# Projecting the last full chunk by tokens in a planned attention and MLP kernel

## The chip, the cores and the metric

The kernel runs on one core of a Trainium2 chip. A core has a matrix engine (PE, with its weight loads shown as PEld), a vector engine (DVE), a scalar engine (ACT), a general engine (POOL), an engine that here only issues transfers (SP), and 16 DMA engines. Each engine works through its own list of instructions in order; semaphores hold an instruction back until what it reads is written and what it overwrites has been read. The metric is the device time of one execution in microseconds, as the median of several runs.

## The reference

Attention with a polynomial feature map comes first, then an MLP whose activation is a rational function:

```python
a = einsum('rd,bhsd->bhsr', S1, x);  b = einsum('rd,bhsd->bhsr', S2, x)
phi(x) = outer product of a and b, flattened            # 8 x 8 = 64 features
kv  = einsum('bhsf,bhsd->bhfd', phi(k), v);  z = phi(k).sum(over s)
x   = (phi(q) @ kv) / (phi(q) . z + 1e-6)               # per head, heads joined: (4352, 128)
h = x @ w_in                                            # (4352, 2048)
P = a[0] + a[1]*h + a[2]*h**2 + a[3]*h**3
Q = 1 + |b[0]|*|h| + |b[1]|*h**2
out = (P / (Q + 1e-6)) @ w_out                          # (4352, 128)
```

There are 4 batches of 4 heads with 1088 tokens and a head width of 32. q, k, v, w_in and w_out are float32; w_in is 128 x 2048 and w_out 2048 x 128. The output is float32.

## The kernel before

**Chunks.** Of each batch 1024 tokens are worked on in two chunks of 512. The first chunk of batch 0 is split into 128 and 384 tokens. The 64 tokens left over in each batch make one last chunk of 256, the remainder. In the loops these are n = 0 to 9: n = 8 is the last full chunk (batch 3, second half) and n = 9 the remainder. In the names of steps the label runs one lower: `0`, `0b`, `1` to `7` for n = 0 to 8, and `8` for the remainder.

**Attention.** For each batch the keys are transposed and turned into features, and PE sums them with the values (L498). For each chunk the queries are transposed (`q tr`), copied (`q ev`), projected (`q abc`), divided by the denominator on DVE (`q dpr`, `q dsum`, `q dinv`, `q scale`), multiplied out (`q prod`), transposed again (`qp tr`), copied (`qp ev`) and multiplied with the sums (`x mm`, L685). The copy `x ev` (L729) gives xT, 128 features by the chunk's tokens.

**MLP.** The 2048 hidden units are 16 blocks of 128. A group g is some blocks of one chunk: n = 7 has groups 15 and 16, n = 8 groups 17 and 18, each of 8 blocks, that is 128 x 4096 values; the remainder has groups 19 to 22 with 8, 4, 3 and 1 blocks. The steps of a group, by their names in the plan:

- `h g,s`: PE multiplies w_in with xT in float32 (L831), two blocks of 512 tokens (four of 256) into one of two PSUM buffers `h_ps`. s counts the blocks, so (18,4) is the third pair of group 18.
- `hev g,s`: the cast of that buffer to bfloat16 `hb` (L838), by ACT, or by DVE for the pairs that CASTS names.
- `abs` (L850), `sq` (L858), `odd` (L862), `oddt` (L868 with hb): DVE makes |h|, h squared, a3 h^2 + a1, and that times h. What is added (`+Q`, `+P`) is added by DVE (L920) or by accumulating DMAs that POOL issues (L924), as PLANS says.
- `ln` (L872) and `exp` (L875): ACT takes Ln of the denominator and Exp of its negative, so u = 1/Q.
- `n5` (L868 with u): DVE multiplies y with u.
- `pr` and `py`: PE multiplies with w_out and adds up in the one PSUM buffer `out_ps`. For groups 13 to 22 the constant a0 is not added to y; instead u itself is projected with w_out scaled by a0 (`w_out_0`), that is `pr`, and y with the other scaled copy (`w_out_b`), that is `py`.

**The two forms of the projection.** Line 888 holds w_out still and streams 512 tokens, so the result has tokens in columns. It is copied (`oev`, L893), transposed by PE (`otr`, L898), copied again (`otev`, L903) and stored. By tokens (L883) the values of 128 tokens are held still and 128 columns of w_out are streamed, so the result has its tokens in partitions; one copy (L957) and the store follow. BY_TOKEN lists the chunks that do it so: here the remainder alone.

**Scaling w_out.** w_out is loaded as float32 into a buffer of the ring `y`. ACT makes w_out_b from it in two halves (`w1`, L435), DVE makes w_out_0 in two halves (`w0`, L436).

**Order.** Every step is entered in a plan with an engine, an estimated duration, what it comes after, a rank, and buffers that it takes and gives back. The planner (`listed`) once put the steps in an order by these numbers; that order is written out as ORDER, and `issue` follows it. Estimated durations, ranks, lags and buffer counts therefore act only through ORDER: each engine's instructions are issued in it. Buffers are handed out in that order too.

**Fillers.** HOT lists groups of matmuls of zeros (L1049) whose result nobody reads. They take a `w_ps` buffer like a transpose, and stand in PE's list where ORDER has them.

Of the kernel before, what the change touches and what calls it, by code (L numbers as in the profile page):

```python
# [55 lines left out]


class Plan:
# [66 lines left out]
def kernel(  # L125
# [37 lines left out]
    BY_TOKEN = (9,)  # L163
# [19 lines left out]
    plan = Plan(BUFS)  # L183
# [87 lines left out]
    ld = {}  # L271
# [813 lines left out]
```

## Time and profile before

| | us |
|---|---|
| median of 3 runs (246.26 to 246.79) | 246.72 |
| the profiled execution | 247.33 |
| its span, first to last instruction | 245.3 |
| busy in the span: PE (weight loads apart) | 239.0 |
| DVE | 223.5 |
| ACT | 219.8 |
| POOL | 48.4 |
| PE in zero matmuls of L1049, 49 of them | 11.8 |

Busy time of PE counts from the start of a matmul to a modelled end. Rows of the timeline merge instructions of one kind: start, time from the start of the first to the end of the last, engine, line, operation, output and inputs, shape, count. Two rows of one engine may overlap by a tenth or more, since an instruction begins before the one ahead has ended; what one costs its engine is therefore taken from start to start. The chain of waits is followed back from the last instruction, at each step to what released it.

### The profile page before, as it was taken

What the parts mean: (1) busy time and instruction counts of PE and PEld (TensorE: products, weight loads), DVE (VectorE), ACT (ScalarE), POOL (GpSimd) and SP (SyncE); (2) the same over time, 40 slices, a digit from 0 to 9 for tenths busy, and PEclk for the clock granted to TensorE, in tenths of its full rate; (3) what the DMA queues carried; (4) which work ended last, traced back from release to release, by engine and by line L of the source; (5) the groups of instructions that cost most, each with busy time, mean ns of one, the idle gap of its engine ahead of it and who ended that gap; (6) DMA issues with size and microseconds to landing.
All of it is one profiled execution on the core that took longest, in us unless ns stands there. A gap on an engine that the chain in (4) does not pass through costs nothing.

```text
span 245.3 us, 3066 instructions
## 1 busy us (share of the span) xinstructions
PE 239.0 (97%) x1148; PEld 138.4 (56%) x1148; DVE 223.5 (91%) x242; ACT 219.8 (90%) x199; POOL 48.4 (20%) x70
## 2 busy tenths in 40 slices
PE   8998999999999999999999999999999999999986
PEld 4887667665556486456464554435444444755453
DVE  0747889999999999999999999999999999999792
ACT  3237799898979998899999999999999999999993
POOL 7800021010121503011112111231311112111100
PEclk9999999999999999999999999999999999999999
DMA  6897706855869999999799999999999999999822
GB/s 159 266 319 178 259 12 123 165 169 97 150 117 184 174 191 222 212 196 179 128 181 180 184 175 176 229 170 187 184 187 191 212 191 172 193 194 188 158 88 64
DMA packets 22206, 42.96 MB, mean 175 GB/s; under 512 B 5536, under 2 KB 12720, under 8 KB 22064
## 3 DMA queue, kind: packets, MB, share of 16 engines
q0 software_dynamic: 8544, 31.74, 72.6%
q1 hardware_dynamic: 13360, 10.95, 14.6%
q8 instruction: 9, 0.15, 0.2%
q10 hardware_dynamic: 288, 0.08, 0.2%
q14 instruction: 5, 0.04, 0.0%
HBM read 8.82 MB, written 2.23 MB: 45 GB/s over the span
## 4 chain that ended last, share of the span: by engine, by line
PE 60%; ACT 35%; issue 3%; DVE 0%; ACTq 0%
PE h_ps L831 31%; ACT u L875 13%; ACT L L872 12%; PE w_ps L498 7%; ACT hb L838 6%; PE out_ps L888 4%; PE w_ps L463 3%; PE w_ps L627 3%; PE w_ps L685 2%; PE w_ps L673 2%; PE w_ps L617 2%; PE w_ps L454 1%; PE out_ps L359 1%; ACT q_pT L679 1%; ACT o_sb L893 1%
## 5 line engine op out<-in xcount | busy, mean ns | idle before, releaser
L831 PE MATMUL h_ps<-xT,w_in_sb 128*128 128x512 f32 (+3 forms) x320 | 126.3, 533 | 0.0
L831 PEld LDWEIGHTS h_ps<-xT,w_in_sb 128*128 128x128 f32 x320 | 55.5, 190 | 41.9 <-issue 31.9
L872 ACT ACTIVATE L<-u,kappa 128x4096 f32<-128x4096 bf16 (+6 forms) x23 | 66.2, 2884 | 0.1
L875 ACT ACTIVATE u<-L 128x4096 bf16<-128x4096 f32 (+6 forms) x23 | 64.3, 2801 | 0.1
L838 ACT CAST hb<-h_ps 128x1024 bf16<-128x1024 f32 (+3 forms) x53 | 54.5, 1051 | 4.8 <-PE h_ps L831 4.6
L924 POOL DMA_DIRECT2D u<-lin x17 | 20.8, 1224 | 120.4 <-DVE lin L858 29.0
L868 DVE TENSOR_TENSOR y<-y,u 128x4096 bf16<-128x4096 bf16 (+6 forms) x23 | 39.7, 1727 | 1.7 <-ACT u L875 1.6
L868 DVE TENSOR_TENSOR y<-y,hb 128x4096 bf16<-128x4096 bf16 (+6 forms) x23 | 39.5, 1725 | 0.0
L858 DVE TENSOR_TENSOR lin<-hb 128x4096 bf16<-128x4096 bf16 (+6 forms) x22 | 37.9, 1724 | 1.4 <-ACT hb L838 1.3
L888 PE MATMUL out_ps<-y,w_out_b 128*128 128x512 bf16 (+2 forms) x144 | 30.6, 355 | 0.2 <-DVE y L868 0.2
L924 POOL DMA_DIRECT2D y<-lin x15 | 19.0, 1268 | 59.5 <-DVE lin L865 27.0
L862 DVE TENSOR_SCALAR y<-lin,a_t 128x4096 bf16<-128x4096 bf16 (+6 forms) x23 | 24.6, 1068 | 0.3 <-ACT lin L856 0.2
L850 DVE TENSOR_SCALAR u<-hb 128x4096 int16<-128x4096 int16 (+6 forms) x23 | 21.6, 941 | 2.1 <-ACT hb L840 1.2
L888 PEld LDWEIGHTS <-w_out_b 128*128 128x128 bf16 x144 | 13.5, 98 | 16.0 <-issue 4.2
L498 PEld LDWEIGHTS w_ps<-v_aug,k_p 128*128 128x128 f32 x128 | 14.9, 192 | 1.4 <-ACT ab L470 0.8
L498 PE MATMUL w_ps<-v_aug,k_p 128*128 128x96 f32 x128 | 15.6, 276 | 0.0
L838 DVE CAST hb<-h_ps 128x1024 bf16<-128x1024 f32 x11 | 13.4, 1220 | 0.7 <-PE h_ps L831 0.7
L865 DVE TENSOR_SCALAR lin<-lin,a_t 128x4096 bf16<-128x4096 bf16 (+3 forms) x13 | 13.4, 1030 | 0.0
L673 PEld LDWEIGHTS w_ps<-ident,q_p 128*128 128x128 f32 x66 | 7.8, 141 | 7.5 <-issue 3.9
L1049 PE MATMUL w_ps<-const-float32-0.0 128*128 128x512 bf16 x49 | 11.8, 381 | 0.0
L679 ACT COPY q_pT<-w_ps 128x512 f32<-128x512 f32 (+2 forms) x18 | 10.9, 603 | 1.0 <-PE w_ps L673 1.0
L888 PE MATMUL out_ps<-u,w_out 128*128 128x512 bf16 x48 | 11.3, 379 | 0.0
(118 smaller groups left out, 226.6 us busy)
## 6 DMA issues: line engine op xcount, KB each, us to landing
u<-lin POOLq DMA_DIRECT2D x14, 1024.0 KB, 8.6
y<-lin POOLq DMA_DIRECT2D x13, 1024.0 KB, 9.5
v_aug<-in_v_dram SPq DMA_DIRECT2D x8, 256.0 KB, 4.9
out_dram<-oT SPq DMA_DIRECT2D x7, 256.0 KB, 7.5
kq<-in_k_dram SPq DMA_DIRECT2D x3, 512.0 KB, 4.7
kq<-in_q_dram SPq DMA_DIRECT2D x3, 512.0 KB, 7.7
u<-lin POOLq DMA_DIRECT2D x2, 768.0 KB, 7.0
w_in_sb<-in_moe_w_in_dram SPq DMA_DIRECT2D x1, 1024.0 KB, 6.6
```

The lines of the kernel that those rows point to most:

```text
L498: nc.tensor.matmul(kv_of((hp,))[:, 0], lhsT=lhs(hp), rhs=rhs(hp), start=(first and hp == hps[0]), stop=final, skip_group_check=True)
L831: nc.tensor.matmul(T["h", g, s][:, i * step:i * step + W], lhsT=w_in_sb[:, fi * 128:(fi + 1) * 128], rhs=T["xT", n][:, :W], start=True, st ...
L838: copy(out=T["t", g][:, s * W:(s + nsub) * W], in_=T["h", g, s][:, :nsub * W])
L850: nc.vector.tensor_scalar(out=u().bitcast(mybir.dt.int16), in0=ht().bitcast(mybir.dt.int16), scalar1=0x7FFF, scalar2=None, op0=AX.bitwise_and)
L858: nc.vector.tensor_mul(out=sq(), in0=ht(), in1=ht())
L862: nc.vector.tensor_scalar(out=y(), in0=sq(), scalar1=a_t[:, 3:4], scalar2=a_t[:, 1:2], op0=AX.mult, op1=AX.add)
L865: nc.vector.tensor_scalar(out=sq(), in0=sq(), scalar1=a_t[:, 0:1], scalar2=None, op0=AX.add)
L868: return lambda: nc.vector.tensor_mul(out=out(), in0=in0(), in1=in1())
L872: nc.scalar.activation(out=T["L", g][:, :gw], in_=u(), func=ACT.Ln, bias=1.0 + 1e-6, scale=kappa[:, 2:3])
L875: nc.scalar.activation(out=u(), in_=T["L", g][:, :gw], func=ACT.Exp, scale=-1.0)
L888: nc.tensor.matmul(T["o", n][:, :W], lhsT=w[:, fi, :], rhs=T[src, g][:, i * W:(i + 1) * W], start=(start and i == 0), stop=(stop and i == ...
L924: nc.gpsimd.dma_start(out=dst(), in_=src(), accum_op=AX.add, max_dma_last_dim=GW)
```

## The change

The full chunk n = 8 joins the remainder in BY_TOKEN. Its four projections (pr and py of groups 17 and 18) become 32 matmuls of 128 columns each, where they were 8 of 512; the copy to o_sb and four transposes behind them fall away, and one copy from `out_ps` takes the place of the copy from the transposes. One more cast, the second half of group 19, goes from ACT to DVE. The scalings of w_out come later in the order, because the planner now counts 700 ns more for the load; a `free u` step tells the planner that u is free once n5 and pr have read it. HOT has the same places but for the last three, 6, 4, 2 where 4, 4, 6 were, 47 matmuls of zeros where 49 were. All steps have new numbers, and ORDER is a new plan for them: the order differs on PE, DVE and ACT from about 16 us on, on SP only in the last stores, and on POOL in one place.

```diff
--- before.py
+++ after.py
@@ -17,42 +17,42 @@
 ORDER = [
-    0, 4, 5, 56, 2, 7, 9, 51, 6, 11, 1, 52, 53, 3, 13, 70, 8, 10, 54, 57, 15, 75, 71, 17, 12, 72, 59, 55, 58, 76,
-    14, 60, 19, 77, 21, 73, 16, 74, 23, 99, 80, 78, 25, 100, 18, 81, 101, 79, 27, 82, 102, 85, 20, 83, 61, 84, 29,
...
-    790, 800, 791, 788, 801, 723, 792]
+    0, 4, 5, 57, 2, 7, 9, 52, 6, 11, 1, 53, 54, 3, 13, 71, 8, 10, 55, 58, 15, 76, 72, 17, 12, 73, 60, 56, 59, 77,
+    14, 61, 19, 78, 21, 74, 16, 75, 23, 100, 81, 79, 26, 101, 18, 82, 102, 80, 28, 83, 103, 86, 20, 84, 62, 85, 30,
...
+    794, 681, 795, 791, 682, 793, 805, 703, 796, 806, 797]
@@ -158,10 +158,10 @@
     FIRST = [4, 4, 8]
     LAST = [8, 4, 3, 1]
     PLANS = {**{g: "QP" for g in range(4, 20)}, **{g:"QPz" for g in range(13,20)},5:"QP",3:"Q",4:"sQP",17:"Qz",19:"QPz",20:"z",21:"z",22:"z"}
-    CASTS = {18:(6,),16:(6,),14:(6,),12:(6,),17:(6,),13:(6,),15:(6,),11:(6,),10:(6,),8:(6,),9:(6,)}
+    CASTS = {18:(6,),16:(6,),14:(6,),12:(6,),17:(6,),13:(6,),15:(6,),11:(6,),10:(6,),8:(6,),9:(6,),19:(4,)}
     PACKED = (0, 9)
-    BY_TOKEN = (9,)
-    HOT = [6, 2, 5, 5, 6, 11, 4, 4, 6]
+    BY_TOKEN = (8,9)
+    HOT = [6, 2, 5, 5, 6, 11, 6, 4, 2]
     ZEROS = 8
     assert d_model == 128 and H == 4 and D == 32 and R == 8 and REM == 64 and J % JC == 0
 
@@ -286,6 +286,7 @@
     ld["q", 0, 1] = load("SP", lambda e: load_main(e, "q_sb", q, 0, 1), 256, rank=-94)
     second = dict(mains(1))
     ld["wo"] = load("SP", load_wo, 800, rank=-93, take=["y"])
+    ld["wo"] = plan.add("ST", 1, lambda: None, after=[ld["wo"]], rank=-93, lag=700, name="w_out")
     ld["k", 1] = load("SP", second["k"], 512, 1, rank=-91, take=["kq"])
     ld["v", 1] = load("SP", second["v"], 512, NP, rank=-90, take=["v_aug"])
     ld["q", 1] = load("SP", second["q"], 512, 1, rank=-89, take=["kq"])
@@ -946,8 +947,10 @@
         p = used(add_up("+P", y, sq, [p, v, dq0], g - 0.3, give=give("sq")), "sq")
         p = used(plan.add("DVE", tt, mul(y, y, u), after=[p, e], rank=g + 0.55, give=[] if z else give("u"), name=f"n5 {g}"), "u")
         o = plan.add("PE", len(fis) * pw, lambda: project("y", w_out_b, first and not z, final), after=[p, rt] + c_w[:1 + (fis[-1] >= NF // 2)], rank=g + 0.56,
-                     take=["out_ps"] if first and not z else [], give=give("u", "y") if z else give("y"), name=f"py {g}")
+                     take=["out_ps"] if first and not z else [], give=give("y"), name=f"py {g}")
         used(o, "y")
+        if z and not packed:
+            plan.add("ST", 1, lambda: None, after=[p, rt], rank=g + 0.56, give=["u"], name=f"free u {g}")
         if packed and final:
             for kind, (tag, _, eng, _) in KINDS.items():
                 plan.add(eng, 1, lambda: None, after=T[kind, "used", n], rank=g + 0.6, give=[tag], name=f"give {tag} {n}")
```

66 rows, old and new, of the table ORDER are left out of this document.

## The prediction

> **What bounds the kernel now.** I read the busy shares first, then the chain of waits, then the stages, then each engine's rows in order of time.
>
> ```profile
> span 245.3 us, 3066 instructions
> ...
> PE 239.0 (97%) x1148; PEld 138.4 (56%) x1148; DVE 223.5 (91%) x242; ACT 219.8 (90%) x199; POOL 48.4 (20%) x70
> ...
> PE 60%; ACT 35%; issue 3%; DVE 0%; ACTq 0%
> ```
>
> Three engines are over 89% busy, so no one of them is "the" bound. The chain lies on PE and then on ACT. The stages say the same (columns: stretch, its length, busy time of PE, weight loads, DVE, ACT and POOL with instruction counts, granted clock, DMA share, GB/s):
>
> ```profile
> 180.00:200.00 20.00, 20.00 (x70) 9.07 (x69) 19.70 (x14) 20.00 (x13) 3.54 (x3) 1.00 1.05 197
> ...
> 225.00:230.00 5.00, 5.00 (x26) 2.33 (x24) 3.74 (x4) 5.00 (x4) 0.86 (x1) 1.00 0.86 160
> ...
> 235.00:240.00 5.00, 3.85 (x55) 3.33 (x56) 4.82 (x12) 4.97 (x8) 0.00 (x0) 1.00 0.15 56
> ```
>
> From 180 to 200 us PE and ACT are full and DVE lacks 0.30 us. At 225 to 230 DVE has 1.26 us free, and at 235 to 240 PE, though its clock stays at 1.00. So work taken from one engine is worth something only as far as the other two come earlier too, and a gap that is worth filling exists on DVE near the end.
>
> **The change, part by part.** The span is 245.3 us; this execution took 247.33, of which 2.03 lie around the span. The median of the runs is 246.72, 0.61 less; the changes below are put on the median.
>
> *Projection by tokens.* Chunk 8 has four projections (pr and py of groups 17 and 18). Each was 8 matmuls of 512 columns and becomes 32 of 128. PE rows near the end show both kinds (columns here and below: start, duration, engine, line and operation, operands and shape, count; in brackets the idle time before and what ended it):
>
> ```profile
> 228.14 1.89 PE L888 MATMUL out_ps<-y,w_out_b 128*128 128x512 bf16 x8
> 229.87 0.60 PE L898 MATMUL w_ps<-ident,o_sb 128*128 128x128 f32 x4
> 230.31 1.89 PE L888 MATMUL out_ps<-u,w_out 128*128 128x512 bf16 x8
> ...
> 235.87 1.06 PE L883 MATMUL out_ps<-w_out,u 128*128 128x128 bf16 x16
> 236.77 1.06 PE L883 MATMUL out_ps<-w_out_b,y 128*128 128x128 bf16 x16
> ```
>
> Start to start, 8 of the long ones take 1.73 us (228.14 to 229.87) and 16 of the short ones 0.90 (235.87 to 236.77), 56 ns each. So 128 short ones take 7.2 us where 32 long ones took 6.9: +0.3 us. The four transposes (229.87 to 230.31) go: -0.44. For PE that is nothing, if the 56 ns hold; the upper bound is one weight load for each matmul, unhidden:
>
> ```profile
> L883 PEld LDWEIGHTS <-u 128*128 128x128 bf16 x32 | 1.9, 98 | 0.8 <-ACT u L875 0.8
> ```
>
> At 98 ns a projection takes 3.1 us and the four 5.6 more than now. I take the 56, because it was measured on these very operands; 98 is kept for a rival. The Trainium skill, page "TensorE: Matmul & The Clock Gate", section "Back-to-back issue gap", gives about 81 ns sustained at 128 columns and about 131 at 512; by it the edit would cost 128 x 81 - 32 x 131 ns, an estimate of +6.2 us on PE. The trace has 56 and 216 ns instead, so the sum does not use it.
>
> *ACT at the end.* These rows stand for the copies and casts that go or move:
>
> ```profile
> 203.10 1.27 ACT L838 CAST hb<-h_ps 128x1024 bf16<-128x1024 f32 x1
> 204.01 0.64 ACT L729 COPY xT<-w_ps 128x256 f32<-128x256 f32 x1
> 204.27 3.99 ACT L872 ACTIVATE L<-u,kappa 128x4096 f32<-128x4096 bf16 x1
> 207.89 0.85 ACT L903 COPY oT<-w_ps 128x512 f32<-128x512 f32 x1
> 208.35 3.90 ACT L875 ACTIVATE u<-L 128x4096 bf16<-128x4096 f32 x1
> ...
> 216.38 1.29 ACT L838 CAST hb<-h_ps 128x1024 bf16<-128x1024 f32 x1
> 217.27 3.92 ACT L875 ACTIVATE u<-L 128x4096 bf16<-128x4096 f32 x1
> ...
> 229.73 0.58 ACT L903 COPY oT<-w_ps 128x512 f32<-128x512 f32 x1
> ...
> 234.76 0.57 ACT L893 COPY o_sb<-out_ps 128x512 f32<-128x512 f32 x1
> 235.22 0.38 ACT L838 CAST hb<-h_ps 128x256 bf16<-128x256 f32 x1
> ...
> 240.53 0.57 ACT L903 COPY oT<-w_ps 128x512 f32<-128x512 f32 x1
> 241.33 0.37 ACT L957 COPY oT<-out_ps 128x256 f32<-128x256 f32 x1 [0.23 <-PE out_ps L883]
> ```
>
> Taken start to start: the cast of group 19's second half (216.38 to 217.27) goes to DVE, -0.89; the o_sb copy of chunk 8 (234.76 to 235.22) goes, -0.46; and of the two late oT copies one still stands behind the last Exp (240.53), now that of chunk 7, so the last store of 256 KB leaves as late as before. SP has the same loads and stores in the same order, but for the stores of the last two full chunks, which change places; POOL moves two pairs of its accumulating DMAs past each other. I cost both at nothing: the output of 240.53 landed within the span's last 4 us and the same bytes go then.
>
> *DVE at the end.* It gets that cast:
>
> ```profile
> 206.41 1.21 DVE L838 CAST hb<-h_ps 128x1024 bf16<-128x1024 f32 x1
> ...
> 224.72 0.54 DVE L862 TENSOR_SCALAR y<-lin,a_t 128x1024 bf16<-128x1024 bf16 x1
> 225.18 2.28 DVE L868 TENSOR_TENSOR y<-y,u 128x4096 bf16<-128x4096 bf16 x1
> ...
> 229.86 2.29 DVE L868 TENSOR_TENSOR y<-y,u 128x4096 bf16<-128x4096 bf16 x1 [1.26 <-ACT u L875]
> ...
> 240.66 0.29 DVE L868 TENSOR_TENSOR y<-y,u 128x256 bf16<-128x256 bf16 x1 [0.29 <-ACT u L875]
> ```
>
> A cast of this shape takes 1.21 us here, 1.14 of it net. It is to fill the 1.26 us that DVE waits at 229.86 for the Exp of group 18 (the n5 product of that group).
>
> *Scalings of w_out later.* DVE stood 2.27 us at the first one, because the load had not landed; behind it stood the denominators and the query product of chunk 0b, which PE transposes next, after a gap of its own:
>
> ```profile
> 17.98 0.75 DVE L436 TENSOR_SCALAR w_out<-y,a_sb 128x1024 bf16<-128x1024 f32 x1 [2.27 <-DMA y<-in_moe_w_out_dram]
> ```
>
> ```profile
> 20.89 0.52 PE L673 MATMUL w_ps<-ident,q_p 128*128 128x128 f32 x3 [0.74 <-ACT kT L458]
> ```
>
> DVE now does the denominators first. PE runs almost without a gap from here on, so whatever DVE wins, PE wins between 0 and its 0.74 us. The row names an ACT copy as what ended the gap, but the new order puts chunk 1's query matmuls into that place, so I take the 0.74 and keep the 0 for a rival. Both ACT scalings of w_out now stand one behind the other, after the xT copy at 24.78 and ahead of the cast at 27.15, where only one stood:
>
> ```profile
> 24.78 0.48 ACT L729 COPY xT<-w_ps 128x384 f32<-128x384 f32 x1 [0.68 <-PE w_ps L685]
> ...
> 25.63 1.16 ACT L435 ACTIVATE w_out_b<-y,a_c 128x1024 bf16<-128x1024 f32 x1
> 27.15 0.80 ACT L840 CAST hb<-h_ps 128x768 bf16<-128x768 f32 x1 [0.35 <-PE h_ps L831]
> ```
>
> That is 1.16 us more in a stretch with 0.35 us of waiting, while the copy itself can come 0.74 earlier: 0.1 us late, which PE's two h_ps buffers cover. If the copy comes no earlier it is 0.8 late, and PE's next pair waits about as long.
>
> *Fillers and the order.* The whole order is planned anew. The zero matmuls (L1049) that come ahead of the remainder's x matmul (202.99) were 6; they are 18 (6, 2, 5, 5), all issued in PE's queue whether PE has time or not.
>
> ```profile
> 156.34 1.09 PE L673 MATMUL w_ps<-ident,q_p 128*128 128x128 f32 x8 [0.46 <-DVE q_p L665]
> ...
> 165.35 1.47 PE L1049 MATMUL w_ps<-const-float32-0.0 128*128 128x512 bf16 x6
> 166.66 1.88 PE L831 MATMUL h_ps<-xT,w_in_sb 128*128 128x512 f32 x4
> ```
>
> ```profile
> 201.18 1.88 PE L831 MATMUL h_ps<-xT,w_in_sb 128*128 128x512 f32 x4
> 202.99 0.72 PE L685 MATMUL w_ps<-q_pT,kv_bd 128*64 128x64 f32 x16
> 203.64 1.98 PE L831 MATMUL h_ps<-xT,w_in_sb 128*128 128x512 f32 x4
> ```
>
> Six take 1.31 us (165.35 to 166.66), so 0.22 each. The one wait of PE that its rows show between 21 and 203 us is the 0.46 at 156.34, and the first 6 of the new fillers stand just ahead of it. Ahead of the last cast of group 18 that ACT makes stand 13 fillers instead of 6, +1.5 us; less 0.74 and 0.46 PE is 0.3 late: its third pair of h matmuls, done at 202.99, would be done at 203.3. The order of these pairs also turns: PE makes (18,4) and then (18,2), ACT takes (18,2) first. So ACT cannot take both until 203.4, and the Ln of group 16 starts at 203.4 + 2 x 0.91 = 205.2. If the fillers all fall into gaps, it starts at 204.0, since the xT copy of the remainder now stands behind it.
>
> *Sum.* From that Ln to the end of group 18's Exp ACT took 229.73 - 204.27 = 25.46 us; less 0.89 (cast), less 0.46 (oT copy at 207.89, now later), plus 0.26 (xT copy) is 24.37. The Exp ends at 228.4 to 229.6. DVE: the cast at 206.41 starts between 204.9 (PE 0.7 early) and 206.9 (12 fillers, 2.6 us, less 1.2, behind the h matmuls of 203.64); from there to the n5 product it took 23.45 us; less the wait of 1.26, less 0.46 (the y of group 20 at 224.72, now later), plus 1.14 is 22.9: 227.8 to 229.8. The later of the two engines decides: 228.4 to 229.8 against 229.86, in the middle 0.75 us earlier. From there DVE carries the end: 11.1 us as before, plus 0.46, less its last wait of 0.29, so +0.17. **Sum: -0.6 us, 246.1 us** (245.4 to 246.8 for this case).
>
> **Rivals.**
> - *The fillers stand in PE's way (slower).* Speaks for it: PE full from 180 to 200, and 12 more filler matmuls ahead of the remainder's x matmul. If neither the 0.74 nor the 0.46 is won back, the Ln of group 16 starts at 206.4, the Exp ends at 230.8, 0.9 to 1.1 later than now; with the 0.17 it is 247.9 us. The sign turns to slower from a start of 205.2, and measurably from 205.7. Against it: PE's matmul ends are modelled, so some of its full stages may hold waits that the rows don't show.
> - *The early start is carried through.* DVE loses its 2.27 us wait, PE is 0.74 ahead throughout and the fillers fall into waits: Exp at 228.4 less 0.74, end 1.3 + 0.7 earlier with the 0.17 counted, 244.8 us. Against it: 0.46 us is all the waiting that PE shows, and 12 fillers cost 2.6.
> - *Each weight load shows (98 ns; slower).* The four projections then take 12.5 us instead of 6.9. py 17 starts at 228.1 now; 0.7 earlier, with 1.4 more for pr 17 ahead of it and three times 3.1 from there, py 18 ends near 238.2. ACT's oT copy of chunk 8 waits for it, and stands in ACT's order ahead of the Ln of group 20, where ACT arrives near 234.1 (234.76, less 0.7). ACT stalls 4.1 us, and the end comes at 250.2 us. It decides from about 70 ns on. Against it: the 56 ns.
> - *PE's clock falls.* The last three fillers (12) now stand behind the last projection, none between py 18 and there. At 235 to 240 us PE idled 1.15 of 5 and kept 1.00. At half speed the last 4 short matmuls and the 12 before them would take 0.9 us more, of which the waits for Exp hide about half: 246.5. The same page of the Trainium skill, section "Why this matters for your kernels", warns of PE gaps over about 3 us between bursts; py 18 ends near 233 and pr 19 follows the Exp of group 19 near 234, so by it nothing happens.
>
> **How the numbers follow.** What this kernel's measurement can tell from no change is 0.2%, 0.5 us. The sum's case has 0.46, of it 0.33 faster and 0.13 same, since its own range crosses that bound; the early start carried through 0.16 (faster); fillers in the way 0.30 (0.27 slower, 0.03 same); weight loads 0.05 (slower); the clock 0.03 (same). That is 0.49 faster, 0.19 same, 0.32 slower. The range reaches to the ends of the two large rivals, 244.8 to 247.9, and leaves out the weight loads.
>
> **What would show it.** In the changed profile: no wait for w_out on DVE before 20 us; short matmuls of out_ps at 56 ns; one more cast on DVE and one o_sb copy fewer on ACT; no DVE wait over 0.5 us at the n5 product of group 18; that product starting at 228.4 to 229.8. Wrong would be: PE's fillers followed at once by h matmuls that ACT waits for (the first rival), or ACT idle ahead of the oT copy of chunk 8 (the third).

## The result, and the profile after

| | before | after |
|---|---|---|
| median of the runs, us | 246.75 (246.26 to 246.89) | 248.47 (248.41 to 249.22) |
| profiled execution, us | 247.33 | 248.41 |
| its span, us | 245.3 | 246.5 |

The ratio of after to before is 1.0068, 95% interval 1.0047 to 1.009: the change costs 1.7 us. The forecast was 246.1, a gain of 0.6; the time lies above its range.

The page after, with the busy shares and the chain of waits by engine:

```profile
span 246.5 us, 3252 instructions
...
PE 238.2 (97%) x1238; PEld 142.0 (58%) x1238; DVE 225.8 (92%) x243; ACT 218.5 (89%) x197; POOL 49.1 (20%) x70
...
PE 77%; DVE 12%; DMA 4%; SPq 3%; issue 2%; ACT 1%; DVEq 0%
```

ACT lost 1.3 us of busy time and DVE gained 2.3, of it 1.2 the cast; but ACT has all but left the chain and DVE and a DMA have come in. The stretches tell where ACT went. Columns as in the prediction (the fourth pair is ACT's busy time); first before, then after:

```profile
20.00:85.00 65.00, 64.26 (x314) 39.68 (x312) 61.02 (x73) 58.58 (x68) 10.36 (x8) 1.00 0.70 143
85.00:155.00 70.00, 70.00 (x318) 40.00 (x315) 69.47 (x58) 67.34 (x55) 12.68 (x11) 1.00 1.00 185
155.00:204.00 49.00, 48.54 (x180) 22.10 (x178) 48.66 (x35) 49.00 (x36) 11.34 (x10) 1.00 1.03 191
```

```profile
20.00:85.00 65.00, 65.00 (x324) 41.15 (x323) 60.69 (x72) 61.05 (x68) 8.33 (x7) 1.00 0.71 147
85.00:155.00 70.00, 69.80 (x306) 39.15 (x305) 69.44 (x59) 65.06 (x54) 13.81 (x11) 1.00 0.99 178
155.00:204.00 49.00, 49.00 (x177) 22.43 (x176) 48.83 (x35) 48.18 (x36) 12.23 (x10) 1.00 1.01 188
```

Up to 85 us the new order gets 2.47 us more out of ACT. From 85 to 155, where PE and DVE are full, ACT gives 2.28 of it back in waiting, and from 155 to 204, where before it had no gap at all, it waits 0.82. So a lead on one engine was built where another engine would take it away again.

The end, in the rows of after, ACT first, then DVE, then PE:

```profile
168.78 1.01 ACT L839 CAST hb<-h_ps 128x1024 bf16<-128x1024 f32 x1 [0.82 <-PE h_ps L832]
...
205.87 3.71 ACT L873 ACTIVATE L<-u,kappa 128x4096 f32<-128x4096 bf16 x1
...
226.71 3.62 ACT L876 ACTIVATE u<-L 128x4096 bf16<-128x4096 f32 x1
230.23 0.35 ACT L839 CAST hb<-h_ps 128x256 bf16<-128x256 f32 x1
```

```profile
207.35 1.23 DVE L839 CAST hb<-h_ps 128x1024 bf16<-128x1024 f32 x1 [0.25 <-PE h_ps L832]
...
219.88 1.22 DVE L839 CAST hb<-h_ps 128x1024 bf16<-128x1024 f32 x1
...
230.47 2.29 DVE L869 TENSOR_TENSOR y<-y,u 128x4096 bf16<-128x4096 bf16 x1
...
241.60 0.29 DVE L869 TENSOR_TENSOR y<-y,u 128x256 bf16<-128x256 bf16 x1
```

```profile
203.53 1.25 PE L1052 MATMUL w_ps<-const-float32-0.0 128*128 128x512 bf16 x5
204.72 0.69 PE L686 MATMUL w_ps<-q_pT,kv_bd 128*64 128x64 f32 x16
205.33 1.98 PE L832 MATMUL h_ps<-xT,w_in_sb 128*128 128x512 f32 x4
...
236.69 1.05 PE L884 MATMUL out_ps<-w_out,u 128*128 128x128 bf16 x16 [1.48 <-ACT oT L960]
```

The moved cast (219.88) fills what was DVE's wait of 1.26 us: the n5 product of group 18 now starts without one, at 230.47, and DVE has no wait to speak of from 207.35 on. But its stretch starts late: the Ln of group 16 at 205.87 (204.27 before), the cast of group 18 at 207.35 (206.41). That cast waits for the h matmuls of 205.33, and five fillers stand two rows ahead of them on PE.

**A scale for all runs.** After the first 20 us an execution repeats itself, so I cut every profile at three DVE rows: the n5 product of group 5, the cast (18,6), and the last product (85.94, 206.41 and 240.66 before; 86.26, 207.35 and 241.60 after). The runs are those of the next section.

| run | start to n5 of group 5 | to the cast (18,6) | to the last product | rest | profiled execution | median |
|---|---|---|---|---|---|---|
| before | 85.94 | 120.47 | 34.25 | 6.67 | 247.33 | 246.72 |
| after | 86.26 | 121.10 | 34.25 | 6.80 | 248.41 | 248.47 |
| a_cast | 86.04 | 121.10 | 35.58 | 7.04 | 249.76 | 249.60 |
| a_notok | 85.49 | 121.11 | 34.78 | 6.80 | 248.17 | 248.22 |
| a_order | 85.75 | 121.11 | 36.08 | 6.81 | 249.74 | 249.44 |
| a_hot | 85.87 | 120.57 | 34.45 | 6.76 | 247.65 | 247.73 |
| a_hotpos | 85.58 | 121.49 | 36.75 | 7.08 | 250.90 | 250.91 |
| b_cast | 85.36 | 120.48 | 34.20 | 6.76 | 246.81 | 246.49 |
| b_token | 85.16 | 120.46 | 33.71 | 11.50 | 250.83 | 251.97 |
| b_tok2 | 86.02 | 120.47 | 34.10 | 6.85 | 247.44 | 246.75 |
| b_tok2cast | 85.49 | 120.47 | 35.10 | 6.77 | 247.83 | 247.70 |
| b_hotpos | 85.17 | 122.10 | 34.62 | 6.58 | 248.47 | 248.49 |
| x_early | 85.80 | 123.01 | 34.14 | 6.71 | 249.65 | 249.53 |
| x_late | 85.19 | 122.11 | 35.11 | 6.81 | 249.22 | 249.78 |
| x_tail | 86.10 | 122.16 | 34.90 | 6.55 | 249.71 | 249.99 |
| x_tail_o | 85.11 | 122.15 | 36.11 | 6.39 | 249.76 | 249.76 |
| b_wout | 85.82 | 120.47 | 34.20 | 6.70 | 247.18 | 246.61 |
| b_swap | 85.36 | 120.46 | 34.06 | 6.73 | 246.61 | 246.56 |
| b_swapwout | 85.43 | 120.47 | 33.98 | 6.68 | 246.56 | 246.78 |
| b_best | 84.99 | 120.47 | 34.17 | 6.78 | 246.41 | 246.54 |

The second column repeats to 0.02 us wherever the order of that stretch is the same. The first varies by over 1 us between executions; a run's median, less the other three columns, gives its usual value: 85.3 before, 86.3 after, 85.4 to 86.0 for the kernels with the changed order but for single steps (a_cast, a_notok, a_order, a_hot, a_hotpos). So of the 1.7 us about 1.0 arises before 86 us in the changed kernel, 0.63 up to the cast (18,6), nothing up to the last product, and 0.13 behind it. The five others have the same order up to 86 us and lose only 0.1 to 0.6 there, so part of the 1.0 is chance in the four executions and not the order's.

That the third column is 34.25 before and after does not mean that nothing changed in it. By a_order, a_notok and a_cast the new order costs 1.83 us there, the cast wins 1.30 to 1.33 of them back and the form by tokens 0.50 to 0.53, where the sum had 0.89 and 0.46.

### The profile page after: what moved, and what is told of

Its sections match the earlier page's. It is cut to its first block, busy times and chain, and to the rows that moved or that the text cites. A ratio compares the mean times of both kernels' runs of the same rounds, so it can differ in the third digit from the quotient of the medians.

```text
span 246.5 us, 3252 instructions
## 1 busy us (share of the span) xinstructions
PE 238.2 (97%) x1238; PEld 142.0 (58%) x1238; DVE 225.8 (92%) x243; ACT 218.5 (89%) x197; POOL 49.1 (20%) x70
## 4 chain that ended last, share of the span: by engine, by line
PE 77%; DVE 12%; DMA 4%; SPq 3%; issue 2%; ACT 1%; DVEq 0%
PE h_ps L832 44%; PE out_ps L889 10%; DVE y L869 6%; PE w_ps L499 5%; DMA kq<-in_k_dram 4%; PE w_ps L686 3%; PE w_ps L674 3%; PE w_ps L628 3%; PE w_ps L1052 3%; PE w_ps L464 2%; DVE lin L859 2%; DVE y L921 1%; DVE y L863 1%; PE w_ps L455 1%; SPq L230 1%
## 5 line engine op out<-in xcount | busy, mean ns | idle before, releaser
L873 ACT ACTIVATE L<-u,kappa 128x4096 f32<-128x4096 bf16 (+6 forms) x23 | 65.3, 2840 | 0.0
L876 ACT ACTIVATE u<-L 128x4096 bf16<-128x4096 f32 (+6 forms) x23 | 63.2, 2749 | 0.2
L839 ACT CAST hb<-h_ps 128x1024 bf16<-128x1024 f32 (+3 forms) x52 | 51.0, 1006 | 5.9 <-PE h_ps L832 5.9
L925 POOL DMA_DIRECT2D u<-lin x17 | 21.4, 1261 | 118.5 <-DVE u L851 47.4
L925 POOL DMA_DIRECT2D y<-lin x15 | 18.2, 1216 | 62.0 <-DVE lin L866 33.8
L889 PE MATMUL out_ps<-y,w_out_b 128*128 128x512 bf16 (+2 forms) x128 | 27.0, 352 | 0.0
L889 PEld LDWEIGHTS <-w_out_b 128*128 128x128 bf16 x128 | 12.2, 100 | 12.8 <-issue 2.9
L839 DVE CAST hb<-h_ps 128x1024 bf16<-128x1024 f32 x12 | 14.6, 1214 | 0.3 <-PE h_ps L832 0.3
L482 DVE TENSOR_TENSOR k_p<-ab 128x1024 f32<-128x1024 f32 x8 | 9.8, 1236 | 2.1 <-ACT ab L471 2.1
L680 ACT COPY q_pT<-w_ps 128x512 f32<-128x512 f32 (+2 forms) x18 | 10.1, 584 | 0.8 <-PE w_ps L674 0.7
```

The lines of the kernel that those rows point to most:

```text
L839: copy(out=T["t", g][:, s * W:(s + nsub) * W], in_=T["h", g, s][:, :nsub * W])
L873: nc.scalar.activation(out=T["L", g][:, :gw], in_=u(), func=ACT.Ln, bias=1.0 + 1e-6, scale=kappa[:, 2:3])
L876: nc.scalar.activation(out=u(), in_=T["L", g][:, :gw], func=ACT.Exp, scale=-1.0)
L889: nc.tensor.matmul(T["o", n][:, :W], lhsT=w[:, fi, :], rhs=T[src, g][:, i * W:(i + 1) * W], start=(start and i == 0), stop=(stop and i == ...
L925: nc.gpsimd.dma_start(out=dst(), in_=src(), accum_op=AX.add, max_dma_last_dim=GW)
```

## The experiments

Kernels named a_ start from the changed one, b_ from the one before. Lines of a diff without code are steps of ORDER by their names. The expectations say TensorE, VectorE and ScalarE for PE, DVE and ACT. Before had 246.46 to 246.71 us in the same five sets of runs.

### The parts: cast, form by tokens, order

**a_cast**: the changed kernel with the cast back on ACT.

```diff
-    CASTS = {..., 9:(6,),19:(4,)}
+    CASTS = {..., 9:(6,)}
```

> The changed kernel with the cast of group 19's second half back on ACT. If DVE is the bound at the end, it has 1.14 us less to do from 219.9 on and the time falls by 0.5 to 1.1 us, to 247.4 to 248.0. If the fillers and with them ACT's lateness set the end, ACT has 0.9 more to do and the time rises by up to 0.9 us, to 248.5 to 249.4.

249.60 us, ratio 1.012 (1.0098 to 1.0142), a little above the second expectation. In the changed order the cast on DVE is worth 1.1 us by the medians, and 1.33 in the third column, where the start has no part.

**b_cast**: the kernel before with that cast on DVE and nothing else (the reverse diff).

> The kernel before, in its own order, with only the cast of group 19's second half on DVE. By the sum it fills the 1.26 us for which DVE waits at 229.9: ACT 0.9 us earlier at the Exp of group 18, the end 0.3 to 0.7 earlier, 246.0 to 246.4. If DVE is the bound to the end, its wait there is only moved and the end comes 0 to 1.1 us later, 246.7 to 247.9.

246.49 us, ratio 1.0004 (0.9988 to 1.002), between the two expectations: worth nothing there. DVE's gap is filled, but ACT, 0.9 us earlier, meets the accumulating DMA that adds up the denominator of group 18:

```profile
221.52 3.71 ACT L873 ACTIVATE L<-u,kappa 128x4096 f32<-128x4096 bf16 x1 [0.77 <-DMA u<-lin]
```

**b_token**: the kernel before with chunk 8 by tokens, the oT copy left where it was, behind the last Exp.

```diff
-    BY_TOKEN = (9,)
+    BY_TOKEN = (8, 9)
```

> The kernel before, in its own order, with only chunk 8 projected by tokens: its o_sb copy and four transposes fall away, its oT copy stays where it was, behind the last Exp. By the sum ACT has 0.46 us less in the last 6 us and PE 0.1 less: 246.2 to 246.8. If the form of the projection is what costs (weight loads that show, or out_ps that is held until the oT copy behind the last Exp), PE waits for out_ps ahead of group 19 until that copy and the time rises by 3 us or more, to 250 to 253.

251.97 us, ratio 1.0217 (1.0185 to 1.025). The single out_ps buffer is now given back by that copy alone, and the remainder's first projection waits for it. Behind this wait the granted clock is 0.50 from 240 to 242 us. Two lots of 16 short matmuls take 3.16 us from start to start (239.71 to 242.87), where one lot took 0.90 before; that makes about 1.4 of the 5.4 us, an estimate from these rows:

```profile
239.71 1.86 PE L884 MATMUL out_ps<-w_out,u 128*128 128x128 bf16 x16 [5.45 <-ACT oT L958]
```

**b_tok2**: the same with that copy where the o_sb copy stood; **b_tok2cast**: with the cast on DVE as well.

```diff
-    exp 19, ..., oev 7, hev 22,0, ln 20, ..., exp 22, ..., otev 7, store 7
+    exp 19, ..., otev 7, hev 22,0, ln 20, ..., store 7, otev 6
```

> The kernel before with chunk 8 by tokens and nothing else, this time with the oT copy moved to where the o_sb copy stood, behind Exp 19. Theory A: 246.0 to 246.9 us (within 0.2% of before): the 5.4 us of the run with the copy left behind the last Exp were its place and nothing of the form. Theory B: 247.5 to 248.5, since out_ps is still held from the first projection to a copy behind Exp 19.

> The same with group 19's second half cast on VectorE as well: all of the change but its new order (the scalings of w_out and the matmuls that keep the clock stay where they were). Theory A: 245.4 to 246.6 us. Theory B: 247.2 to 248.4. If it is under 246.0 it is shorter than both kernels.

246.75 us (ratio 1.0002, 0.9985 to 1.0019) and 247.70 (1.0047, 1.0022 to 1.0071). In the old order the form by tokens is neutral once the copy is early. Both edits together cost 0.9 us in the third column, which neither costs alone. The time is theory B's, but the cause is not `out_ps`: the product of group 19 waits for the transfer that adds up its y.

```profile
235.67 1.23 DVE L869 TENSOR_TENSOR y<-y,u 128x2048 bf16<-128x2048 bf16 x1 [1.21 <-DMA y<-lin]
```

**a_notok**: the changed kernel with chunk 8 by features again; **a_order**: that, and the cast on ACT, so the new order alone.

```diff
-    BY_TOKEN = (8,9)
+    BY_TOKEN = (9,)
-    exp 19, ..., otev 7, ln 20, exp 20, ..., exp 22, otev 6
+    exp 19, ..., oev 7, ln 20, otev 6, exp 20, otr 7, pr 19, ..., exp 22, otev 7
```

> The changed kernel with chunk 8 projected by features and transposed behind it, as before; its copy o_sb stands where the changed order has the oT copy, its transposes ahead of group 19's first projection, its oT copy behind the last Exp. Theory A (the newly laid order costs the time, the form of the projection nothing): 248.1 to 248.8 us, no nearer to the kernel before. Theory B (the form by tokens costs it, because out_ps is held for the oT copy and group 19's projection waits 1.5 us): 246.6 to 247.3.

> The new order alone: chunk 8 by features as above, and group 19's second half cast on ScalarE as before. Theory A: 249.0 to 249.9 us, as long as the changed kernel without the cast (249.6). Theory B: 247.4 to 248.2.

248.22 us (1.0064, 1.004 to 1.0087) and 249.44 (1.0112, 1.009 to 1.0135). Theory A holds: the new order alone costs 2.9 us, the form by tokens 0.2, less than the runs can tell, and the cast takes 1.2 off. (The third column has the form at -0.53; the medians differ by the start as well.) In the third column the order alone has 1.83 us more than before. ACT is late at Ln 16, and DVE waits for the Exp of group 18:

```profile
231.26 2.29 DVE L870 TENSOR_TENSOR y<-y,u 128x4096 bf16<-128x4096 bf16 x1 [1.91 <-ACT u L877]
```

Counted from the n5 product of group 5, Ln 16 starts at 119.67 us in a_order (205.42), 1.34 later than before. From there to the end of the Exp of group 18 ACT takes 25.71 us, where it took 25.46, with three casts in both orders; a wait of 0.64 us for PE is part of it. So the n5 product of group 18 comes 1.59 later. Behind it DVE takes 11.68 us to the last product instead of 10.80: one step of 0.46 us that stood ahead of that product now stands behind it, and DVE waits 0.55 us for another Exp. Together that is 2.47 us, the 0.64 of the second column and the 1.83 of the third. The granted clock falls to 0.50 from 232 to 234 us in this run, but ACT and DVE show no wait for PE between there and the last product.

### The fillers

HOT holds only the sizes of the lots; where they stand in PE's list is ORDER's matter, and the new plan moved the first five of them.

**a_hot**: 14 of the 18 fillers ahead of the remainder's x matmul taken out of the changed kernel, one left at each place.

```diff
-    HOT = [6, 2, 5, 5, 6, 11, 6, 4, 2]
+    HOT = [1, 1, 1, 1, 6, 11, 6, 4, 2]
```

> The changed kernel with HOT = [1, 1, 1, 1, 6, 11, 6, 4, 2]: 14 of the 18 zero matmuls ahead of the remainder's x matmul taken out, everything else as it is. If the fillers stand in PE's way (the first rival), PE is 14 x 0.22 = 3.1 us less loaded, the Ln of group 16 starts at about 204.3 instead of 205.9, and the time falls to 246.5 to 247.3. If DVE is what is late (it runs without a gap to the end and has one cast more), the time stays within 0.5 us of 248.5.

247.73 us, ratio 1.0047 (1.003 to 1.0064), 0.7 less than after and between the two expectations. But the first of these fillers starts at 155 us, and half of the 0.7 lies in the first column, where they can have no part. Behind it the columns are 0.37 us shorter in sum: 0.53 less in the second, 0.20 more in the third. So 3.1 us of PE work give back about 0.4 us. In the second column they are 0.53 of the 0.63 which the changed order loses there, but Ln 16 hardly moves. It stands 119.46 us behind the n5 product of group 5, where after has 119.61 and before 118.33; the expectation had it at 204.3:

```profile
205.33 3.71 ACT L874 ACTIVATE L<-u,kappa 128x4096 f32<-128x4096 bf16 x1
```

**b_hotpos**: the kernel before, its fillers as many as before, but the first five lots moved to the changed order's places.

```diff
-    h 15,2, hot 0 | pr 15, hot 1 | h 19,4, hot 2, hot 3 | h 21,0, hot 4
+    h 14,4, hot 0 | h 15,2, hot 1 | hot 2, py 12 | hot 3, h 18,4 | h 19,0, hot 4
```

> The kernel before with the same zero matmuls, but the first five lots at the places the changed order gives them (behind h 14,4; behind h 15,2; ahead of py 12; ahead of h 18,4; behind h 19,0). If fillers early on PE delay the casts of group 18 as the first rival says: Ln of group 16 0.5 to 1.5 us later than 118.33 us behind the n5 of group 5, time 247.1 to 247.9. If PE has room for them: within 0.2% of before.

248.49 us, ratio 1.0075 (1.0051 to 1.0099): as slow as the changed kernel by this alone and above the first expectation, with 1.63 us of it in the second column. PE first, then ACT:

```profile
201.74 1.25 PE L1050 MATMUL w_ps<-const-float32-0.0 128*128 128x512 bf16 x5
202.83 1.88 PE L832 MATMUL h_ps<-xT,w_in_sb 128*128 128x512 f32 x4
```

```profile
204.74 1.01 ACT L839 CAST hb<-h_ps 128x1024 bf16<-128x1024 f32 x1 [1.47 <-PE h_ps L832]
205.65 0.38 ACT L730 COPY xT<-w_ps 128x256 f32<-128x256 f32 x1
205.91 3.73 ACT L873 ACTIVATE L<-u,kappa 128x4096 f32<-128x4096 bf16 x1
```

The fillers stand ahead of the h matmuls that ACT waits for; Ln 16 starts at 205.91, as in the changed kernel. This is the first rival's mechanism, shown in the old order.

**a_hotpos**: the reverse, the changed kernel with its fillers at about the old places.

```diff
-    h 14,4, hot 0 | h 15,2, hot 1 | hot 2, py 12 | hot 3, x mm 8 | h 19,0, hot 4
+    h 15,2, hot 0 | pr 15, hot 1 | h 19,4, hot 2, hot 3 | h 21,0, hot 4
```

> The changed kernel with its zero matmuls moved back to about the places of the order before: the lot of 6 behind h 15,2, the 2 behind pr 15, the two lots of 5 behind h 19,4, the next 6 behind h 21,0; their numbers unchanged. In the old order the changed places cost 2.0 us. If they cost the same in the changed order: 246.4 to 246.9 us, as before. If that order has other delays of its own at the same places (cutting 14 of the matmuls gave back only 0.7 us): 247.4 to 247.9.

250.91 us, ratio 1.018 (1.0159 to 1.0201), outside both expectations. The second column stays as long (121.49), and a new wait arises near the end: 16 fillers now stand ahead of py 16, and ACT's o_sb copy waits for py 16 with Ln 18 behind it.

```profile
224.76 0.59 ACT L895 COPY o_sb<-out_ps 128x512 f32<-128x512 f32 x1 [2.79 <-PE out_ps L890]
```

So a place that is harmless in one order is not in the other. That fillers taken out of the changed order give back 0.53 us up to the cast (18,6) is shown; that their places explain that column is not.

### Spliced orders

Four kernels follow one order up to a step and the other from there. **x_early**: the changed order up to n5 7, then before's; **x_late**: the reverse, with cast and form by tokens; **x_tail**: before's up to n5 14, then the changed, with both; **x_tail_o**: that without either.

```diff
 x_early   -  ORDER of before                  +  after's steps up to n5 7, then before's remaining ones
 x_late    -  ORDER of after                   +  before's steps up to n5 7, then after's remaining ones
 x_tail    -  ORDER of after                   +  before's steps up to n5 14, then after's remaining ones
 x_tail_o  -  ORDER of after, by features      +  before's steps up to n5 14, then after's remaining ones
```

> The changed order up to the last product of group 7 (about 99 us), the order of before from there; neither the cast on VectorE nor chunk 8 by tokens. Theory E (the loss is made early: VectorE's short waits and dependent neighbours between 20 and 100 us, 1.07 us more than before, less 0.57 won at w_out): 246.9 to 247.7 us. Theory L (it is made behind 185 us, where Ln 16 starts 1.1 to 1.6 us later): 246.2 to 246.9, as before.

> The other way round: the order of before up to the last product of group 7, the changed order from there, with the cast on VectorE and chunk 8 by tokens as in the changed kernel. Theory E: 246.8 to 247.7 us. Theory L: 248.1 to 248.9, as the changed kernel.

> The same with the seam at the last product of group 14 (about 185 us): all of before's order until then, then the changed order, cast and form by tokens. Theory E: 246.5 to 247.4 us. Theory L: 248.0 to 248.9. If the loss is made between 99 and 185 us: under 247.2 here, over 248 in the run with the seam at group 7.

> The seam at group 14 again, without the cast and without the form by tokens: the end of the new order alone. In the run of the new order alone VectorE took 36.09 us from group 18's cast to its last instruction, against 34.25 before, so theory L: 248.2 to 249.2 us (1.84 of its 2.85 us). Theory E, by which that stretch is longer only because it starts late: 246.4 to 247.4.

249.53, 249.78, 249.99 and 249.76 us (ratios 1.0117, 1.0125, 1.013 and 1.0127, each to about 0.002): all four miss both theories, because each seam makes a wait of its own. From x_early, x_late and x_tail:

```profile
122.52 1.23 DVE L839 CAST hb<-h_ps 128x1024 bf16<-128x1024 f32 x1 [2.56 <-PE h_ps L832]
```

```profile
117.73 1.29 DVE L866 TENSOR_SCALAR lin<-lin,a_t 128x4096 bf16<-128x4096 bf16 x1 [1.61 <-DMA u<-lin]
```

```profile
208.26 1.23 DVE L839 CAST hb<-h_ps 128x1024 bf16<-128x1024 f32 x1 [1.62 <-PE h_ps L832]
```

The totals therefore decide nothing. The stretches still do: behind the seam x_early takes 34.14 us to the last product, as before, and x_tail_o 36.11, as the new order alone (36.08). So the 1.83 us of the third column go with the new order's end, whatever order stands ahead of it.

### The scalings of w_out

**b_wout**: the kernel before with DVE's first scaling behind the query product of chunk 0b and ACT's two next to each other.

```diff
-    w0 1, q dpr 0b, ..., q prod 0b, w0 0
+    q dpr 0b, ..., q prod 0b, w0 0, w0 1
```

> The kernel before with the scalings of w_out later and nothing else: VectorE's first one behind the query product of chunk 0b, ScalarE's two next to each other. Theory S (the start of the kernel hangs on one landing: in the seven runs with before's early order the n5 product of group 5 stands 67.97 to 68.45 us behind the first scaling of w_out, whose load landed between 17.0 and 18.1 us; freed of it the start is as in the runs with the early landing, and the k transposes of batch 1 come next): 246.2 to 246.6 us, 0 to 0.4 less than before, n5 of group 5 near 85.1 us. The prediction's step (0.74 us won): 245.7 to 246.1. If the later scalings themselves are the changed kernel's early loss: 246.9 to 247.5.

246.61 us, ratio 1.0 (0.9984 to 1.0017): the step is worth nothing, and costs nothing.

```profile
17.90 0.26 DVE L649 TENSOR_TENSOR den<-abc 128x96 f32<-128x96 f32 x1 [1.70 <-ACT abc L638]
```

The wait for w_out becomes one of 1.70 us for the query projection, which ACT copies no earlier. That is theory S's range but for a hundredth; that the start would always be an early one (85.1) did not come true (85.82).

### A version with the cast that beats both?

**b_swap**: b_cast with three DVE steps moved; **b_swapwout**: with b_wout's edit too; **b_best**: b_swap with the o_sb copy of chunk 6 put into ACT's wait ahead of Ln 18.

```diff
-    sq 18, odd 18, abs 18 | abs 22, +Q 22, +P 20, odd 22, oddt 22, n5 20, +P 22, +P 21 | ln 18, oev 6, exp 18
+    sq 18, abs 18, odd 18 | abs 22, +P 20, +Q 22, odd 22, +P 21, oddt 22, n5 20, +P 22 | oev 6, ln 18, exp 18
```

> The kernel before with the cast of group 19's second half on VectorE, and three VectorE steps of the end moved so that they don't stand right behind the step whose result they read: abs 18 ahead of odd 18, +P 20 ahead of +Q 22, +P 21 ahead of oddt 22. Theory N (a step behind its own input costs 0.11 to 0.19 us more, and abs 18 coming 1.3 us earlier ends ScalarE's 0.77 us wait for the accumulating DMA at Ln 18 that the cast alone has): 245.7 to 246.2, shorter than both kernels. If ScalarE bounds the end anyway: 246.3 to 246.7.

> Both of these together (scalings of w_out later; cast on VectorE with the three steps moved). Additive: the gain of the one plus the gain of the other, 245.3 to 246.2 us.

> The kernel before with the cast on VectorE, the three VectorE steps moved as above, and the o_sb copy of chunk 6 (0.46 us on ScalarE) ahead of Ln 18 instead of behind it, into the 0.66 us that ScalarE waits there for the accumulating DMA. If ScalarE bounds the end: 246.0 to 246.4 us, 0.3 less than the run without this move, the least of all kernels here. If the DMA's landing decides: no less than 246.4.

246.56 (ratio 0.9994, 0.9977 to 1.0012), 246.78 (1.0008, 0.9994 to 1.0021) and 246.54 (1.0001, 0.9984 to 1.0017): no gain that can be told; the additive 245.3 to 246.2 was missed. The third column falls from 34.20 (b_cast) to 34.06, 33.98 and 34.17, a tenth or two, because in b_best ACT still waits 0.35 us for the DMA at Ln 18 while DVE reaches the product of group 18 without a gap, and at the last product DVE waits for ACT. ACT and DVE end within some tenths of each other, and what one gains meets the other. Nothing here beats the kernel before by more than the runs can tell.

## Why the prediction was wrong

- **The sum's base.** It took its gains from an execution 0.61 us above the median and put them on the median. That execution started late: w_out had landed late. With before's early order the n5 product of group 5 follows DVE's first scaling of w_out by 67.96 to 67.97 us wherever that scaling stood at 17.14 or later. From x_tail_o and x_tail, which share that order (before: 17.98 and 85.94):

```profile
17.14 0.75 DVE L437 TENSOR_SCALAR w_out<-y,a_sb 128x1024 bf16<-128x1024 f32 x1 [1.66 <-DMA y<-in_moe_w_out_dram]
...
85.11 2.28 DVE L869 TENSOR_TENSOR y<-y,u 128x4096 bf16<-128x4096 bf16 x1
```

```profile
18.13 0.75 DVE L437 TENSOR_SCALAR w_out<-y,a_sb 128x1024 bf16<-128x1024 f32 x1 [2.14 <-DMA y<-in_moe_w_out_dram]
...
86.10 2.28 DVE L869 TENSOR_TENSOR y<-y,u 128x4096 bf16<-128x4096 bf16 x1
```

- **"Scalings of w_out later": the 0.74 us of PE.** The wait for w_out went, as said, but PE won nothing. In the changed order PE does a third fewer h matmuls before it transposes the keys of batch 1, so these meet their load: in after the transposes at 19.30 waited 0.45 us for it, and n5 of group 5 came at 86.26; in x_early, same early order, they started at 18.84 and n5 came at 85.80. Both are 66.96 us apart, and in the other five kernels with this early order it is 66.89 to 66.96:

```profile
18.84 0.66 PE L455 MATMUL w_ps<-ident,kq 128*128 128x128 f32 x4 [0.18 <-DMA kq<-in_k_dram]
```

  The chain of waits of after runs through that load, from its start to its landing at 19.25:

```profile
8.95 10.30 DMA kq<-in_k_dram
```

  One landing was exchanged for a later one. That this is all of the early loss is argued from these rows; no run moved the load of the keys.
- **"ACT's scalings 0.1 late, covered"** and the 0 for POOL and SP: nothing in the runs speaks against them (b_wout's total).
- **"13 fillers instead of 6, +1.5 us; less 0.74 and 0.46 PE is 0.3 late", and from it Ln 16.** This is the step that failed. Ln 16 was put at 204.0 to 205.2 and started at 205.87; the cast (18,6) at 204.9 to 206.9 and started at 207.35. Of the two credits the 0.74 was lost to the keys. The other one was there: with the fillers moved away, in a_hotpos, PE waits 0.49 us at that place (155.07), and in after the fillers fill it.

  What was wrong above all is the path to Ln 16. The sum let it wait for PE's third pair of h matmuls, but in after ACT is full from 168.78 us to Ln 16, and it comes to its casts at 203.80 late by itself. Of the 1.28 us by which Ln 16 starts later, counted from the n5 product of group 5, taking out 14 fillers gives back only 0.15, and 0.20 at the two casts ahead of it. ACT idles 2.66 us in this stretch before, 5.81 in after and 5.71 in a_hot; that Ln 16 is not later still comes from the earlier lead, since after has 1.87 us less work for ACT there. So the lateness lies in waits which the new order brought and the sum had at nothing.

  DVE is where the fillers count: they make 0.53 of the 0.63 us by which the cast (18,6) comes later, and in after DVE has no wait from that cast to the last product that could take the delay up. In a_hot a wait of 0.22 us for a DMA uses part of the gain. In the old order the same places cost 2.0.
- **The first rival** had a late Ln 16 (206.4) and 247.9 us with a chance of 0.30, and came closest. That it did is in part luck: its cause, fillers ahead of h matmuls that ACT waits for, is what b_hotpos shows, and in after it holds for DVE's cast but not for ACT.
- **The order's own waits.** "The whole order is planned anew" was priced at its fillers alone. ACT's 2.28 us more of waiting between 85 and 155 us has no filler near it: the first starts at 155.09, and in a_hotpos at 167.75, with the same 65.06 us of ACT work in that stretch. It cancels an earlier lead, and the row of before with PE at 70.00 of 70 was a warning. Which of these waits made Ln 16 late no run took apart.
- **From Ln 16 to the end of group 18's Exp: 24.37 us.** Right: 230.23 - 205.87 = 24.36, to the hundredth by luck. After has a wait of 0.20 us at 222.48 that the sum did not have, and before had 1.33 us from the cast at 220.79 to Ln 18 where a cast costs 0.89.
- **From the cast (18,6) to n5 of group 18: 22.9 us.** 23.12 measured. The moved cast takes 1.32 us from start to start (219.88 to 221.20), because the next step reads it (below); 1.14 was put for it, though in before too the step behind the cast at 206.41 starts 1.31 us later (207.72). The gap was filled, as said, but n5 started at 230.47, outside 228.4 to 229.8, since its stretch started late. From there 11.1 + 0.17 was given relative to before; it took 11.13, where before took 10.80, +0.33.
- **By tokens: 56 ns for a short matmul.** Right: in a_hotpos 32 of them take 1.78 us from start to start.

```profile
227.40 1.95 PE L885 MATMUL out_ps<-w_out,u 128*128 128x128 bf16 x32
229.18 1.95 PE L885 MATMUL out_ps<-w_out_b,y 128*128 128x128 bf16 x32
```

  The 81 ns of the Trainium skill, page "TensorE: Matmul & The Clock Gate", section "Back-to-back issue gap", are not met in this stream of weight loads and matmuls either.

  The third rival (98 ns) is out, and b_tok2 shows the form neutral in the old order. Not foreseen was that by tokens out_ps is held until the oT copy: PE waits 1.48 us at 236.69 in after. There it is hidden, as the later projections wait for DVE; in b_token, where the copy stood behind the last Exp, the time rose by 5.4 us.
- **The clock** stayed at 1.00 in the profile after: the fourth rival is out.

What stays open: how much each wait of ACT between 85 and 169 us adds to the late Ln 16, and how much of the early 1.0 us belongs to the order.

## What to carry to other kernels

Where an order is planned anew, price the whole order and not the edit: add up each engine's waits by stretch, and count a lead on one engine as nothing if the next stretch has another engine full. Fillers are work like any other wherever their engine feeds one that has no gap; the same places cost 2.0 us in the old order and about 0.4 in the new one. And before a gain is put on a median, look for what made the profiled execution differ from it, here one landing at the start.

## What the hardware showed that was not expected

- The start decides by one transfer, and the rest of the execution repeats: the landing of w_out, and with it DVE's first scaling, moved between 16.73 (b_best) and 18.13 us (x_tail), and from 17.14 on everything behind it moved along; the second column of the table agrees to 0.02 us over the nine kernels that share its order.
- A DVE instruction that reads what the one just ahead wrote starts later. In the rows of after, a product that reads the sum ahead of it comes 2.39 us behind that sum; in the rows of before a square that doesn't comes 2.20 us behind a sum of the same size:

```profile
223.28 2.28 DVE L921 TENSOR_TENSOR y<-y,lin 128x4096 bf16<-128x4096 bf16 x1
225.67 2.29 DVE L869 TENSOR_TENSOR y<-y,u 128x4096 bf16<-128x4096 bf16 x1
```

```profile
219.12 2.28 DVE L920 TENSOR_TENSOR y<-y,lin 128x4096 bf16<-128x4096 bf16 x1
221.32 1.22 DVE L858 TENSOR_TENSOR lin<-hb 128x2048 bf16<-128x2048 bf16 x1
```

  That is 0.19 us for each such pair. The Trainium skill, page "VectorE: DVE Perf Modes", section "The DRAIN you can't avoid", has the next operation start only once the pipe is empty, and earlier where it is not held. By the rows here an independent one starts 0.08 us before its predecessor's record ends, and the dependent one 0.11 us behind it.
- PE's granted clock fell to 0.50 for a little over 3 us in five of the profiles, each time about when PE took up work again behind a wait: of 2.13 us (x_tail), 2.34 (x_late), 2.57 (a_order and x_tail_o) and 5.45 (b_token). With waits up to 1.59 us (x_early) it stayed at 1.00, but so it did behind one of 2.50 us in a_cast. The length of the wait alone does not decide it.
